# One load for three inverse tiles, score stacks issued four rounds later, and a late projection in the bank of the sums: a change to a kernel of two attention and two spectral layers

## The chip, the cores and the metric

The kernel runs on one core of a Trainium2 chip. A core has five engines that each work through a queue of their own in order: TensorE (PE in the profile, its weight loads PEld), VectorE (DVE), ScalarE (ACT), GpSimd (POOL) and SyncE (SP). Here SP computes nothing: it issues nearly all transfers between the chip's main memory (DRAM) and the core's own memory. The metric is device time in microseconds (us), the median of several runs. Before the change it is 1366.31 us, from three runs of 1366.28 to 1366.6 us.

## The reference

The input `x` has 2048 tokens of 576 columns. Two kinds of layers alternate, each added to its input: attention in a sliding window of 256 tokens with 32 heads of 18 columns, and a spectral filter (a two-dimensional Fourier transform, a product with a complex filter, the transform back).

```python
def _A_ref(x, wqkv, wo):
    H = 32; Dh = D // H; W = 256
    qkv = (x @ wqkv).reshape(B, S, 3, H, Dh).transpose(2, 0, 3, 1, 4)
    q, k, v = qkv[0], qkv[1], qkv[2]
    scores = jnp.einsum("bhqd,bhkd->bhqk", q, k) * (Dh ** -0.5)
    mask = (idx[:, None] - idx[None, :] >= 0) & (idx[:, None] - idx[None, :] < W)
    p = softmax(jnp.where(mask, scores, -1e9))
    o = jnp.einsum("bhqk,bhkd->bhqd", p, v)
    return o.transpose(0, 2, 1, 3).reshape(B, S, D) @ wo

def _B_ref(x, w_r, w_i):
    X = jnp.fft.rfft2(x, axes=(-2, -1)) * (w_r + 1j * w_i)
    return jnp.fft.irfft2(X, s=(S, D), axes=(-2, -1))

x = A_x
x = x + _A_ref(layernorm(x), A_wqkv, A_wo)
x = x + _B_ref(layernorm(x), B_w_r, B_w_i)
x = x + _A_ref(layernorm(x), A_wqkv, A_wo)
x = x + _B_ref(layernorm(x), B_w_r, B_w_i)
```

Everything is fp32. The kernel splits a number into a high part that TensorE multiplies exactly and a low part, the remainder, and adds the products of the parts.

## The kernel before

**Attention layer.** The 2048 tokens are 16 tiles of 128, the 32 heads are 8 quads of 4. First come the layer norm and the projection of the values (L1005). Then the queries and keys are projected: `proj(i, c)` computes column group `i` (of 9) for token block `c` (of 4, 512 tokens each) in 14 TensorE steps into one bank of PSUM, the memory that TensorE writes its products to. ScalarE copies the high part out (`sg`), and the remainder (`tensor_sub`, L1127) is put in a list `ended`, which `remainders()` empties later on VectorE. After it a DMA (L1129) stores both parts to DRAM (`qk_d`). The bank is free when the remainder is done.

From DRAM they come back arranged for the scores: `stack_load(n, c)` issues 12 loads (L1144, six for queries `qs`, six for keys `ks`) that build the stack of quad `n`, block `c`. There are two buffers, used by even and odd quads in turn.

The work on a quad runs in rounds, one for each of its 16 tiles, 128 rounds in all. A round has four score products (`score_max`, L1169), which VectorE reduces to row maxima (L1171), and, ten rounds later (`LEAD = 10`), four exponent products (`exps`, L1206), which ScalarE turns into probabilities (L1207). GpSimd cuts the window out of them, and TensorE adds up the products with the values (`part`, L1226) in a bank named `U`. After each four rounds `m_rows(n, c)` transposes the maxima, ScalarE negates them (`mt`, L1184), and four small DMAs (L1189) write them as one more row of `qs`, so that the next exponent products of that block subtract them. `norm` divides the sums and stores them (L1251).

**PSUM.** The banks go by tags: three of tag `S` for scores, three of tag `E` for exponent products, one `pj` for projections and one `U` for the sums. In the first ten rounds, the opening, there are no exponent products yet: the projections take turns in `pj` and the `E` banks (column group 2), and the fourth score of a round uses `U`.

**Order.** `opening()` runs ten rounds of scores with 70 projection steps between them. `bursts()` then takes three exponent products and three scores at a time; the projection steps that are left are spread over bursts by the tables `ends` and `unit`, one projection of 14 steps for each entry of `ends`. The first of these is `proj(3, 0)`, in an `E` bank, then `proj(3, 1)`, in `pj`. After 118 rounds (`MIX`) a loop without scores follows.

`loads(t)` runs at the start of round `t` of the exponent products (rounds below are in this count) and issues stacks: those of quad 1 at rounds -4, 4, 8 and 12, those of quads 2 to 7 at every fourth round, with the quad and block of round `t + 20`. `behind(t)` runs after a round, for the layer's end: at round 104 the output weights (`room`, L734, two loads to `ofree`), at rounds 107, 109 and so on the constants of the next stage (`const`, L748, `dc`), later the layer's input rows. All of these stand in SP's one queue, which issues in order; a load that must wait for data holds up those behind it. SP's DMAs signal on eight semaphores in turn, so that each also waits for the eighth before it.

**Spectral layer.** After the forward transform a pipeline of 16 groups `g` applies the filter along the tokens (L496, L517); VectorE and GpSimd write the result `ze`, and each group's rows are stored to DRAM (`yd`, L554). The inverse transform then works through 16 tiles `n2` (L591 and after). Its tile `n2` needs rows of all groups: tiles 0 to 2 get the rows of groups 0 to 10 by loads from `yd` that are issued in groups 10 and 13 (L544, three loads each time, one for each tile), and the rows of later groups straight from `ze` (L524). Tile 3 and later ones are fetched whole from `yd` (`fetch`, L585), and the layer's input is loaded in pairs of tiles (`ld`, L170). All these tiles lie in the room `ofree`, called `rl` in the code; `yis` are its four places for inverse tiles, one behind the other from column 4640 on, and `near` is 3.

Of the kernel before, what the change touches and what calls it, by code (L numbers as in the profile page):

```python
# [136 lines left out]
def layer_b(tc, xf, dst, dcs, gc, ident, rh, rl, out, ga_d, fc_d, m2_d, w_d, wo_d, wo2_d, dram, nxt, share):  # L137
# [10 lines left out]
    with ExitStack() as stack:  # L148
# [361 lines left out]
        def g2(g, h):  # L510
# [30 lines left out]
            if g in (FG - 1, FG + 2):  # L541
                lo, hi = (0, 8) if g < FG else (8, FG)
                for n2 in range(near):
                    nc.sync.dma_start(yis[n2][8 * lo:8 * hi].rearrange("p c f -> p (c f)"), yd[1][n2, lo:hi].rearrange("g i f -> (g i) f"))  # L544
            if g == 14:
# [30 lines left out]
        def ly(n2, h):  # L576
            h["y"] = yis[n2 % 4]
            if n2 == 0:
                ld(4)
            for k in (near,) if n2 == 0 else (n2,) if n2 > near + 1 else ():  # L580
                fetch(k)

        def fetch(k):
            if k >= near:
                nc.sync.dma_start(yis[k % 4].rearrange("p c f -> p (c f)"), yd[1][k].rearrange("g i f -> (g i) f"))  # L585
# [279 lines left out]
def layer_a(tc, ident, eps, bp, src, dst, wqk_d, wv_d, wo_d, dc_d, gc_d, dram, copy, wvs, second, spectral, share):  # L865
# [17 lines left out]
    if True:  # L883
# [192 lines left out]
        with ExitStack() as c2:  # L1076
# [17 lines left out]
            def remainders():  # L1094
                while ended:
                    ended.pop(0)()

            def proj(i, c, bank=0):
# [5 lines left out]
                def mm(s, k):  # L1104
# [3 lines left out]
                    if s == 0:  # L1108
                        box["ps"] = pp.tile([128, 512], F32, tag="E" if bank else "pj", name=f"pj{i}_{c}", bufs=3 if bank else 1)
                    w = wt[i][0] if p == "h" else wt[i][1]  # L1110
# [153 lines left out]
            LEAD = 10  # L1264
            pj = [f for i in range(2, 9) for c in range(4) for f in proj(i, c, c % 2 if i == 2 else c == 0 and i == 3)]
            done, due = 0, []
# [3 lines left out]
            def loads(t):  # L1270
                if t + LEAD in (0, 2):
                    stack_load(0, 2 + (t + LEAD) // 2)
                if t in (-4, 4, 8, 12):
                    stack_load(1, max(t, 0) // 4)
                n, c = divmod(t + 20, NT)
                if c % 4 == 0 and 1 < n < NQ:
# [33 lines left out]
            def bursts():  # L1310
# [4 lines left out]
                values = {(4 * x + 7) // 3 + 2 for x in range(0, MIX - 2, 2)}  # L1315
                ends = [3] + [max(k - 1 for k in values if k - 1 <= 4 + 134 * (i + 1) // 22) for i in range(22)]
                unit = {k: i for i, end in enumerate(ends) for k in range(ends[i - 1] + 1 if i else 0, end + 1)}
# [99 lines left out]
            for f in opening():  # L1417
                f()
                done += 1
            U = pp.tile([128, 512], F32, tag="U", name="U", bufs=1)  # L1420
            V.memset(U, 0.0)
            for f in bursts():
# [96 lines left out]
```

## Time and profile before

| | before |
|---|---|
| median of 3 runs | 1366.31 us |
| the profiled execution, its own time | 1367.9 us |
| its span, first to last instruction | 1366.2 us |
| mean granted TensorE clock | 0.997 |
| TensorE busy, attention layer 1 (0 to 490 us) | 481.6 of 490.0 us |
| TensorE busy, spectral layer 1 (490 to 705 us) | 211.2 of 215.0 us |
| TensorE busy, attention layer 2 (705 to 1186 us) | 473.4 of 481.0 us |
| TensorE busy, spectral layer 2 (1186 to 1366.2 us) | 169.7 of 180.2 us |
| chain that ended last: TensorE / DMA / VectorE / ScalarE | 87% / 4% / 3% / 2% |
| score products (L1169), idle time of TensorE just before them | 1.0 us |
| exponent products (L1206), idle time of TensorE just before them | 6.4 us |

The table's windows come from the view that sums an engine's busy time over a stretch. How to read the rows of the other views:

- A row of the timeline has the start in us, the duration in us, the engine, the line of the kernel, the operation, the tile written and the tiles read, the shapes and how many instructions of one kind stand together (x6). `SPq` is SP's queue: the duration of such a row is the time in which the DMAs were issued, not the time until the data is there. In brackets stands how long the engine had been idle before, and what ended the idle time.
- A row of the table of waits has the engine, the tile and line that waited, what it waited for, and then three numbers: the total in us, the number of waits, and the longest of them. It also sums only waits in a given stretch where one is asked for.
- The granted clock is TensorE's, 1.00 at full speed.

### The profile page before, as it was taken

Reading aid. Unit: us, or ns where it says so; the run is one execution under the profiler, and the core shown is the slowest. Engines: PE = TensorE matmul, PEld = TensorE weight load, DVE = VectorE, ACT = ScalarE, POOL = GpSimd, SP = SyncE. Lnnn points to the kernel's source line nnn. Section 1 sums busy time; section 2 is a strip of 40 time slices with the busy share of each in tenths; the row PEclk is TensorE's granted clock in tenths of the full one; section 3 lists DMA queues with packets and bytes.
Section 4 is the critical chain, followed back from the end, with each engine's and each line's share of the span. In section 5 each row is a group of like instructions: output and inputs, shape, how many; then the busy total and the mean of one; then the engine's idle time right before and its main releaser. Section 6 shows DMA issues by size and latency. Waiting matters only on the chain.

```text
span 1366.2 us, 33609 instructions
## 1 busy us (share of the span) xinstructions
PE 1335.8 (98%) x11351; PEld 997.2 (73%) x11351; DVE 900.5 (66%) x3060; ACT 780.0 (57%) x1966; POOL 644.0 (47%) x1154
## 2 busy tenths in 40 slices
PE   9999999999999999999999999999999999999998
PEld 8986666666665699975999965566666655898587
DVE  5418777877778376666663157777777785576745
ACT  5522777777778544542455316677777778464223
POOL 3257545555546533476221394455455458213721
PEclk9999999999999999999999999999999999999999
DMA  6756665655446457778773467555555555597875
GB/s 204 208 164 194 207 190 166 188 166 160 150 145 180 129 154 249 223 237 266 253 243 73 114 194 224 160 170 162 153 158 153 157 157 168 143 359 253 301 234 173
DMA packets 202425, 259.11 MB, mean 190 GB/s; under 512 B 104599, under 2 KB 109975, under 8 KB 201743
## 3 DMA queue, kind: packets, MB, share of 16 engines
q1 hardware_dynamic: 191551, 235.72, 57.0%
q10 hardware_dynamic: 7648, 14.96, 3.1%
q0 software_dynamic: 3056, 6.28, 1.8%
q8 instruction: 92, 1.51, 0.5%
q14 instruction: 78, 0.64, 0.2%
HBM read 156.11 MB, written 101.01 MB: 188 GB/s over the span
## 4 chain that ended last, share of the span: by engine, by line
PE 87%; DMA 4%; DVE 3%; ACT 2%; issue 2%; SPq 1%; POOL 0%; ACTq 0%; DVEq 0%; POOLq 0%
PE pj L1112 19%; PE S L1169 12%; PE U L1226 12%; PE vps L1005 8%; PE ops L800 7%; PE E L1206 6%; PE po L257 3%; PE pq L517 2%; PE tpo L1240 2%; PE pf L257 2%; PE p L496 2%; PE pi L591 2%; PE pz L295 2%; DMA ofree<-yd 1%; PE tpm L1182 1%
## 5 line engine op out<-in xcount | busy, mean ns | idle before, releaser
L1171 DVE CUSTOM_DVE_ANT_0 jk<-S,mask 128x384 bf16<-128x384 f32 (+2 forms) x1024 | 490.7, 529 | 113.5 <-PE E L1206 60.3
L1207 ACT ACTIVATE P<-E 128x384 f32<-128x384 f32 (+2 forms) x1024 | 409.1, 476 | 128.0 <-PE E L1206 99.2
L1209 POOL TENSOR_SCALAR_AFFINE_SELECT P<-P 128x512 f32<-128x512 f32 x256 | 162.6, 635 | 278.2 <-ACT P L1207 257.3
L1169 PE MATMUL S<-ks,qs 63*128 63x384 f32 (+2 forms) x1024 | 269.1, 371 | 1.0 <-DMA qs<-qk_d 0.4
L1206 PE MATMUL E<-qs,ks 64*128 64x384 f32 (+2 forms) x1024 | 222.4, 372 | 6.4 <-DMA qs<-mt 3.7
L1169 PEld LDWEIGHTS S<-ks,qs 63*128 63x128 f32 x1024 | 140.7, 185 | 105.4 <-DVE m L1171 72.4
L1226 PE MATMUL U<-P,vq 128*19 128x128 f32 (+1 forms) x3840 | 188.3, 329 | 0.6 <-DVE us L1231 0.2
L1112 PE MATMUL pj<-xh,wqh 128*128 128x512 f32 x360 | 156.2, 434 | 1.7 <-DVE sg L1127 1.3
L1226 PEld LDWEIGHTS U<-P,vq 128*19 128x19 f32 x3840 | 96.0, 98 | 77.7 <-issue 25.0
L1212 POOL TENSOR_SCALAR_AFFINE_SELECT P<-P 128x512 f32<-128x512 f32 x224 | 142.3, 635 | 0.0
L1206 PEld LDWEIGHTS E<-qs,ks 64*128 64x128 f32 x1024 | 113.7, 185 | 21.3 <-ACT P L1207 9.7
L1112 PE MATMUL pj<-xh,wql 128*128 128x512 f32 x360 | 124.4, 418 | 0.0
L1112 PE MATMUL pj<-xl,wqh 128*128 128x512 f32 x288 | 122.3, 425 | 0.0
L800 PE MATMUL ops<-oroom 128*128 128x290 f32 (+1 forms) x812 | 115.4, 298 | 0.4 <-DVE ofree L846 0.2
L800 PEld LDWEIGHTS ops<-oroom 128*128 128x128 f32 x812 | 110.2, 189 | 1.1 <-DVE ofree L823 0.7
L1112 PEld LDWEIGHTS pj<-xh,wqh 128*128 128x128 f32 x360 | 67.8, 188 | 32.5 <-issue 10.5
L1171 DVE DVE_READ_ACCUMULATOR2_ANT m<- 128x1 f32 x1024 | 85.3, 83 | 0.0
L1127 DVE TENSOR_TENSOR sg<-pj,sg 128x512 fp32r<-128x512 f32 x72 | 49.5, 687 | 52.5 <-ACT sg L1124 52.5
L1124 ACT CAST sg<-pj 128x512 fp32r<-128x512 f32 x72 | 42.2, 586 | 69.2 <-PE pj L1112 54.2
L1112 PEld LDWEIGHTS pj<-xh,wql 128*128 128x128 f32 x360 | 64.3, 189 | 20.3 <-issue 10.7
L1005 PE MATMUL vps<-wvh,xh 128*128 128x288 f32 x320 | 71.4, 304 | 0.0
L1112 PEld LDWEIGHTS pj<-xl,wqh 128*128 128x128 f32 x288 | 54.3, 189 | 18.3 <-issue 11.6
(599 smaller groups left out, 2257.5 us busy)
## 6 DMA issues: line engine op xcount, KB each, us to landing
qk_d<-sg SPq DMA_DIRECT2D x56, 512.0 KB
qs<-qk_d SPq DMA_DIRECT2D x384, 72.0 KB
ks<-qk_d SPq DMA_DIRECT2D x348, 72.0 KB
v_d<-vt SPq DMA_DIRECT2D x32, 304.0 KB
vq<-v_d SPq DMA_DIRECT2D x16, 608.0 KB
wt<-in_w SPq DMA_DIRECT2D x16, 580.0 KB
ofree<-x SPq DMA_DIRECT2D x16, 580.0 KB
x<-ofree SPq DMA_DIRECT2D x32, 290.0 KB
```

Of the source, the lines that this page charges most:

```text
L257: T.matmul(ps[:, c, 0:NF], tail[r] if si == 4 else hl_(si), dcs[b // 2][r, b % 2], start=mi == si == 0, stop=si == 4)
L800: self.nc.tensor.matmul(self.ps[u][n][:, 0:self.n], x, self.w[p][:, (2 * wk + n) * self.n:(2 * wk + n + 1) * self.n], start=first and i == ...
L1005: T.matmul(ps[:, n, 0:288], xT(xk, c), w[:, wk, n * 288:(n + 1) * 288], start=i == 0, stop=i == len(ks) - 1)
L1112: T.matmul(box["ps"].rearrange("r (n p) -> r n p", n=NT) if second else box["ps"], w[:, wk], x, start=s == 0, stop=s == len(ks) - 1)
L1127: V.tensor_sub(rest[:, 1], by, rest[:, 0].bitcast(F32))
L1169: T.matmul(ps[:, 0:N], q[b:b + 63, pair, i * 128:i * 128 + 128], k[b:b + 63, pair, lo:hi], start=True, stop=True)
L1171: V.tensor_tensor_reduce(out=jk[:, 0:N], in0=ps[:, 0:N], in1=mask[:, 384 - N:384], scale=1.0, scalar=-3e38, op0=ALU.add, op1=ALU.max, accu ...
L1206: T.matmul(ps[:, 0:nq], k[b:b + 64, pair, j * 128:j * 128 + 128], q[b:b + 64, pair, j * 128:j * 128 + nq], start=True, stop=True)
L1207: A.activation(p[:, hl_, 0:nq], ps[:, 0:nq], AF.Exp, scale=SC)
L1209: P.affine_select(out=p[:, :, 0:128], in_=p[:, :, 0:128], pattern=[[0, 4], [1, 128]], compare_op=ALU.is_ge, fill=0.0, base=0, channel_mult ...
L1212: P.affine_select(out=p[:, :, 256:384], in_=p[:, :, 256:384], pattern=[[0, 4], [-1, 128]], compare_op=ALU.is_gt, fill=0.0, base=0, channel ...
L1226: T.matmul(U[32 * h:32 * h + 19, (q0 % 4) * 128:(q0 % 4) * 128 + 128 * (q1 - q0)], vts[n][:, j, h], pt[n, j][:, h, (q0 - j) * 128:(q1 - j) ...
```

## The change

There are four edits. The bulk loads of the first three inverse tiles become one DMA that writes all three tiles (in groups 10 and 13). In the first tile of the inverse transform the fetch of tile 3 is issued ahead of the load of the input pair 4. The projection `proj(3, 0)` goes to the bank `pj` instead of an `E` bank, and `proj(3, 1)` to `U`, which therefore exists earlier, with a `remainders()` ahead of it and without the memset; the first entry of `ends` is 2 instead of 3. The stacks of quads 2 to 7 are those of round `t + 16` instead of `t + 20`.

```diff
@@ spectral layer, group g of the filter along the tokens @@
             if g in (FG - 1, FG + 2):
                 lo, hi = (0, 8) if g < FG else (8, FG)
-                for n2 in range(near):
-                    nc.sync.dma_start(yis[n2][8 * lo:8 * hi].rearrange("p c f -> p (c f)"), yd[1][n2, lo:hi].rearrange("g i f -> (g i) f"))
+                nc.sync.dma_start(rl[8 * lo:8 * hi, 4640:4640 + 580 * near].rearrange("p (n f) -> p n f", n=near),
+                                  yd[1][0:near, lo:hi].rearrange("n g i f -> (g i) n f"))
@@ spectral layer, tile n2 of the inverse transform @@
             h["y"] = yis[n2 % 4]
+            for k in (near,) if n2 == 0 else (n2,) if n2 > near + 1 else ():
+                fetch(k)
             if n2 == 0:
                 ld(4)
-            for k in (near,) if n2 == 0 else (n2,) if n2 > near + 1 else ():
-                fetch(k)
@@ attention layer, proj @@
-                        box["ps"] = pp.tile([128, 512], F32, tag="E" if bank else "pj", name=f"pj{i}_{c}", bufs=3 if bank else 1)
+                        box["ps"] = U if bank == 2 else pp.tile([128, 512], F32, tag="E" if bank else "pj", name=f"pj{i}_{c}", bufs=3 if bank else 1)
@@ attention layer, the list of projection steps @@
-            pj = [f for i in range(2, 9) for c in range(4) for f in proj(i, c, c % 2 if i == 2 else c == 0 and i == 3)]
+            pj = [f for i in range(2, 9) for c in range(4) for f in proj(i, c, c % 2 if i == 2 else 2 if (i, c) == (3, 1) else 0)]
@@ attention layer, loads @@
-                n, c = divmod(t + 20, NT)
+                n, c = divmod(t + 16, NT)
                 if c % 4 == 0 and 1 < n < NQ:
                     stack_load(n, c // 4)
@@ attention layer, bursts @@
-                ends = [3] + [max(k - 1 for k in values if k - 1 <= 4 + 134 * (i + 1) // 22) for i in range(22)]
+                ends = [2] + [max(k - 1 for k in values if k - 1 <= 4 + 134 * (i + 1) // 22) for i in range(22)]
@@ attention layer, between opening and bursts @@
             for f in opening():
                 f()
                 done += 1
+            remainders()
             U = pp.tile([128, 512], F32, tag="U", name="U", bufs=1)
-            V.memset(U, 0.0)
             for f in bursts():
```

Three places show how this moves the loads in SP's queue. In the rows, a number behind a tile's name numbers its buffer, and `x4` says how many instructions of one kind stand together.

The first place is SP's queue in the first attention layer, rounds 12 to 16. `mt1_0` is the row of maxima of quad 1, block 0, which is written to the odd quads' buffer `qs1`; `qs1`/`ks1` from `qk_d` are a stack of quad 1, `qs0`/`ks0` a stack of quad 2; `sg3_3` is the store of a projection. Before:

```order
L1189 DMA qs1_1060<-mt1_0_2134 1x4x128 x4
L1144 DMA qs1_1060<-qk_d_83 18x2x512 x6
L1144 DMA ks1_1061<-qk_d_83 18x2x512 x6
L1144 DMA qs0_1058<-qk_d_83 18x2x512 x6
L1144 DMA ks0_1059<-qk_d_83 18x2x512 x6
L1129 DMA qk_d_83<-sg3_3_2228 128x2x512
L1251 DMA o_d_85<-o0_2_2311 128x4x72
L1189 DMA qs1_1060<-mt1_1_2342 1x4x128 x4
```

With the change:

```order
L1189 DMA qs1_1060<-mt1_0_2132 1x4x128 x4
L1144 DMA qs1_1060<-qk_d_83 18x2x512 x6
L1144 DMA ks1_1061<-qk_d_83 18x2x512 x6
L1129 DMA qk_d_83<-sg3_3_2214 128x2x512
L1251 DMA o_d_85<-o0_2_2297 128x4x72
L1189 DMA qs1_1060<-mt1_1_2328 1x4x128 x4
L1144 DMA qs0_1058<-qk_d_83 18x2x512 x6
L1144 DMA ks0_1059<-qk_d_83 18x2x512 x6
```

The first stack of quad 2 has moved from ahead of the row `mt1_1` to behind it, past a store of a projection and one of an output.

The second place is SP's queue at the end of the same layer, rounds 104 to 111, where the last stacks are those of quad 7. `ofree` from `in_wo` are the output weights, `dc0` and `dc1` the first two constants, `mt7_0` and `mt7_1` the rows of maxima of quad 7, `o6_1` an output. Before:

```order
L1144 DMA qs1_1060<-qk_d_83 18x2x512 x6
L1144 DMA ks1_1061<-qk_d_83 18x2x512 x6
L734 DMA ofree_7004<-in_wo 128x1152
L734 DMA ofree_7004<-in_wo 128x1728
L1189 DMA qs1_1060<-mt7_0_7098 1x4x128 x4
L1251 DMA o_d_85<-o6_1_7140 128x4x16
L1251 DMA o7_d_86<-o6_1_7140 128x4x56
L748 DMA dc0_7144<-dcr_62 128x580
L748 DMA dc1_7239<-dcr_62 128x580
L1189 DMA qs1_1060<-mt7_1_7273 1x4x128 x4
```

With the change:

```order
L1144 DMA qs1_1060<-qk_d_83 18x2x512 x6
L1144 DMA ks1_1061<-qk_d_83 18x2x512 x6
L734 DMA ofree_6990<-in_wo 128x1152
L734 DMA ofree_6990<-in_wo 128x1728
L1189 DMA qs1_1060<-mt7_0_7084 1x4x128 x4
L1251 DMA o_d_85<-o6_1_7126 128x4x16
L1251 DMA o7_d_86<-o6_1_7126 128x4x56
L748 DMA dc0_7130<-dcr_62 128x580
L1144 DMA qs1_1060<-qk_d_83 18x2x512 x6
L1144 DMA ks1_1061<-qk_d_83 18x2x512 x6
L748 DMA dc1_7237<-dcr_62 128x580
L1189 DMA qs1_1060<-mt7_1_7271 1x4x128 x4
```

The stack ahead of the weights is now the last but one; the last stack stands between the constants `dc0` and `dc1`, ahead of the row `mt7_1`.

The third place is SP's queue in the first spectral layer, where the filter along the tokens ends and the inverse transform begins. `yd1` is the DRAM tensor of the stored rows, `eo2`, `ze13`, `eo3` and `ze15` are rows of groups 12, 13, 14 and 15, and `x0` is the layer's input. Before:

```order
L524 DMA ofree_7004<-eo2_8122 8x580 x2
L544 DMA ofree_7004<-yd1_8102 24x580 x3
L524 DMA ofree_7004<-ze13_10155 8x580
L524 DMA ofree_7004<-eo3_8123 8x580
L524 DMA ofree_7004<-ze15_10188 8x580 x2
L554 DMA yd1_8102<-ze13_10155 16x8x580
L554 DMA yd1_8102<-ze15_10188 16x8x580
L170 DMA ofree_7004<-x0_59 128x1160 x2
L585 DMA ofree_7004<-yd1_8102 128x580 x2
```

With the change:

```order
L524 DMA ofree_6990<-eo2_8120 8x580 x2
L543 DMA ofree_6990<-yd1_8100 24x3x580
L524 DMA ofree_6990<-ze13_10151 8x580
L524 DMA ofree_6990<-eo3_8121 8x580
L524 DMA ofree_6990<-ze15_10182 8x580 x2
L554 DMA yd1_8100<-ze13_10151 16x8x580
L554 DMA yd1_8100<-ze15_10182 16x8x580
L170 DMA ofree_6990<-x0_59 128x1160
L585 DMA ofree_6990<-yd1_8100 128x580
L170 DMA ofree_6990<-x0_59 128x1160
L585 DMA ofree_6990<-yd1_8100 128x580
```

Three loads of group 13 have become one, and the fetch of tile 3 (the first L585) stands ahead of the second load of input rows instead of behind it.

## The prediction

> **What bounds the kernel now.** I read the page first, for its share of busy time, then the table of waits for TensorE, then TensorE's granted clock in short windows, and last the timeline of SP (the queue that issues nearly every transfer) at each place where TensorE stood still.
>
> ```profile
> span 1366.2 us, 33609 instructions
> PE 1335.8 (98%) x11351; PEld 997.2 (73%) x11351; DVE 900.5 (66%) x3060; ACT 780.0 (57%) x1966; POOL 644.0 (47%) x1154
> ```
>
> TensorE is busy for 98% of the span, so 30.4 us of idle time is all that an edit of order can win there, and the change removes no matmul. The waits, longest first:
>
> ```profile
> PE E L1206 <- DMA qs<-mt: 3.7, 2, 2.5
> PE pi L591 <- DMA ofree<-ze: 3.4, 2, 2.0
> PE pi L591 <- DMA ofree<-yd: 2.0, 2, 1.5
> ```
>
> Each is one event in each layer: the exponent products wait for a row of maxima, the inverse transform waits for its last rows and then for its fourth tile. Two of these waits have a tail, which only the clock shows (columns: window, busy time of PE, PEld, DVE, ACT, POOL, then granted clock, DMA share, GB/s):
>
> ```profile
> 643.20:647.00 3.80, 3.80 (x15) 3.24 (x14) 2.24 (x5) 0.00 (x0) 1.39 (x6) 0.56 0.97 301
> 879.40:882.70 3.30, 3.30 (x25) 1.58 (x23) 1.61 (x6) 1.33 (x4) 1.03 (x2) 0.52 0.64 201
> ```
>
> At a clock of 0.56 the first stretch loses 3.80 x 0.44 = 1.7 us, the second 3.30 x 0.48 = 1.6 us. They are the only such stretches while TensorE works, and each follows a gap of 2.0 us or more (rows below).
>
> **Term 1, stacks four rounds later.** In round 12 SP issues two stacks, 24 loads, ahead of the four small loads that carry a row of maxima. In the second layer:
>
> ```profile
> 865.38 3.21 SPq L1144 DMA_DIRECT2D qs<-qk_d  x6
> 868.63 3.29 SPq L1144 DMA_DIRECT2D ks<-qk_d  x6
> ...
> 873.50 2.73 SPq L1189 DMA_DIRECT2D qs<-mt  x4
> ...
> 866.39 0.27 ACT L1184 ACTIVATE mt<-tpm 16x128 fp32r<-16x128 f32 x1
> ...
> 877.26 0.90 PE L1206 MATMUL E<-qs,ks 64*128 64x384 f32 x3 [2.49 <-DMA qs<-mt]
> ...
> 179.01 1.03 PE L1206 MATMUL E<-qs,ks 64*128 64x384 f32 x3 [1.21 <-DMA qs<-mt]
> ```
>
> The row was ready at 866.66 and was issued 6.8 us later, behind the second stack of 6.5 us. With that stack in round 16 the row leaves some 6.5 us earlier, more than both waits: 2.49 + 1.21 = 3.7 us gone, and with the gap the stretch at half clock, 1.6 us. Together **5.3** (bounds 3.7 to 5.3). Round 16 then holds one stack, as it does now.
>
> **Term 2, the projections' banks.** The last projection of the opening sat in one of the three E banks until VectorE had taken its remainder:
>
> ```profile
> 128.90 0.44 PE L1206 MATMUL E<-qs,ks 64*128 64x384 f32 x1 [0.68 <-ACT P L1207]
> 131.62 0.44 PE L1206 MATMUL E<-qs,ks 64*128 64x384 f32 x1 [0.44 <-ACT P L1207]
> ...
> 130.37 0.69 DVE L1127 TENSOR_TENSOR sg<-pj,sg 128x512 fp32r<-128x512 f32 x1
> ...
> PE E L1206 <- ACT P L1207: 1.0, 2, 0.5
> ```
>
> Until 131.06 only two E banks turned; that cost 1.1 us here and 1.0 us (the last row, the waits between 780 and 835 us) in the second layer. Now this projection has the pj bank and the next one the bank of sums, so three turn at once. The remainder moves ahead of the round's reductions on VectorE, which delays each score by up to 0.69 us; three S banks cover that. The bank of sums must be read out before the sums start, a whole burst after the projection ends. Bounds 0 to 2.1; I take **1.7**, near the upper end, since the buffer that was lacking is there. The memset that goes was hidden behind TensorE.
>
> **Term 3, the inverse transform, first layer.** SP is the chain here: three loads, then four short ones, the last two with the rows that the first inverse product needs.
>
> ```profile
> 635.20 2.28 SPq L544 DMA_DIRECT2D ofree<-yd  x3
> ...
> 639.08 1.38 SPq L524 DMA_DIRECT2D ofree<-ze  x2
> ...
> 637.13 0.45 DVE L529 TENSOR_TENSOR ze<-pq,both 128x290 f32<-128x290 f32 x1
> ...
> 642.31 0.97 PE L591 MATMUL pi<-ofree,ga 128*128 128x290 f32 x3 [2.00 <-DMA ofree<-ze]
> ```
>
> One load in place of three takes no less than one of them (2.28 / 3 = 0.76) and no more than all three; I take 0.8, as SP's time goes by instructions in these rows. Then 1.5 us are free, but the last rows can't leave before VectorE has written them at 637.58: 639.08 - 637.6 = 1.4 us won. The gap of 2.00 falls to 0.6 us, shorter than any that the half clock followed, so its 1.7 us go too: **3.1** (bounds 0 to 3.7).
>
> **Term 4, the same place in the second layer.**
>
> ```profile
> 1295.35 1.21 SPq L544 DMA_DIRECT2D ofree<-yd  x3
> ...
> 1298.15 1.33 SPq L524 DMA_DIRECT2D ofree<-ze  x2
> ...
> 1296.81 0.45 DVE L529 TENSOR_TENSOR ze<-pq,both 128x290 f32<-128x290 f32 x1
> ...
> 1302.30 0.97 PE L591 MATMUL pi<-ofree,ga 128*128 128x290 f32 x3 [1.38 <-DMA ofree<-ze]
> ...
> 1305.14 0.80 SPq L585 DMA_DIRECT2D ofree<-yd  x2
> ...
> 1310.77 0.51 PE L591 MATMUL pi<-ofree,ga 128*128 128x290 f32 x1 [1.54 <-DMA ofree<-yd]
> ```
>
> Three take 1.21, so 0.8 is saved, and VectorE's rows are ready at 1297.26: 0.8 of the 1.38 goes. The fourth tile landed 5.6 us after its issue, with two loads of 580 KB ahead of it; one of them now stands behind it, which at this place's pace is worth more than the 1.54 us waited. I take 1.2 of 1.54, since it must still wait for the last store. **2.0** (bounds 0 to 2.9). In the first layer this load has slack.
>
> **Term 5, what the shift costs.** The last stack of a layer moves from ahead of the output weights' loads (L734) to between the first two constants, and so ahead of the next row of maxima:
>
> ```profile
> 416.73 2.12 SPq L1144 DMA_DIRECT2D qs<-qk_d  x6
> 418.89 2.35 SPq L1144 DMA_DIRECT2D ks<-qk_d  x6
> 421.33 0.84 SPq L734 DMA_DIRECT2D ofree<-in_wo  x2
> ...
> 427.99 2.33 SPq L748 DMA_DIRECT2D dc<-dcr  x2
> 430.42 2.44 SPq L1189 DMA_DIRECT2D qs<-mt  x4
> ...
> 434.75 1.21 PE L1206 MATMUL E<-qs,ks 64*128 64x384 f32 x3
> ...
> 1129.90 2.51 SPq L748 DMA_DIRECT2D dc<-dcr  x2
> 1132.51 2.44 SPq L1189 DMA_DIRECT2D qs<-mt  x4
> ...
> 1135.46 1.06 PE L1206 MATMUL E<-qs,ks 64*128 64x384 f32 x3
> ```
>
> The second constant waits until the weights have landed, about 430; twelve loads take 4.5 us, and they will stand there too. Part returns: the stack at 416.73 had waited 2.2 us for the last projection's store; its successor, with other columns, needs it only at its sixth load, so the weights come some 1.8 us sooner (in the second layer 1.1). So the four small loads are 2.7 us late in the first layer and 3.4 in the second. Their slack is read from the rows: issued by 432.86 and used at 434.75, 1.9 us; by 1134.95 and used at 1135.46, 0.5 us. In term 1's rows TensorE went on 1.0 us after the last issue (876.23 to 877.26). So 0.9 us are spare in the first layer and none in the second: waits of 1.8 and 3.4 us, queued ahead of every later score, product and sum, since TensorE takes them in order. The longer one may bring a half-clock stretch of 1.6 us; at even chance 0.8. Loss **6.0** (bounds 0 to 10.6: no lead returned, both clocks halved).
>
> **Sum.** 5.3 + 1.7 + 3.1 + 2.0 - 6.0 = 6.1 us off the span of 1366.2: 1360.1. The median, 1366.31, lies 0.1 above this span (the profiled execution itself took 1367.9), so the forecast is **1360.2** for the median.
>
> The Trainium skill (TensorE: Matmul & The Clock Gate, Part 1) has the clock halve after an idle window of about 3.4 us. In these rows gaps of 2.00 and 2.49 us were enough and 1.38 and 1.54 were not; I go by the rows. By the page's figure the two gaps would be too short to cause the stretches.
>
> **Rivals.**
> (a) The stack at the end of the layer is hidden, its load landing sooner than the rows say: term 5 is zero, 1366.3 - 12.1 = 1354.2. For it: slack exists in the first layer; against: 0.5 us in the second.
> (b) One load of three tiles holds SP as long as three did: terms 3 and 4 shrink to the 1.2 us of the order of loads, 1366.3 - 8.2 + 6.0 = 1364.1. The change then doesn't do what it says. For it: issues in those rows differ from 0.40 to 0.76 us each, so their cost is not understood.
> (c) The half-clock stretches have another cause and stay: 3.3 us less, 1363.5. For it: the second begins 2.1 us after its gap has ended.
> (d) Term 5 is paid in full, 10.6 us, in both layers: 1366.3 - 12.1 + 10.6 = 1364.8.
> (e) The other side: the stacks come too late for their scores, at all 24 of a layer.
>
> ```profile
> 295.38 2.23 SPq L1144 DMA_DIRECT2D qs<-qk_d  x6
> ...
> 319.95 0.44 PE L1169 MATMUL S<-ks,qs 63*128 63x384 f32 x1
> ...
> 337.92 2.42 SPq L1144 DMA_DIRECT2D qs<-qk_d  x6
> ```
>
> Stack (5,0) starts at 295.38 and is first read at 319.95; sixteen rounds take 42.5 us (to 337.92), so four take 10.6, and 14 us are left, of which 4.5 are issue. It decides once SP lags or a load lands 9 us later than it seems. Then each of 48 stacks waits, at 0.5 us each 24 us: 1366.3 - 12.1 + 24 = 1378. Against it: SP had gaps there and the margin is twice the issue.
>
> **Numbers.** Forecast 0.58, with its own range 1356.5 to 1363.4; (a) 0.14, (b) 0.08, (c) 0.06, (d) 0.06, (e) 0.08. A measurement of this kernel tells about 0.2%, 2.7 us, from no change. The forecast, (a) and (c) are faster by more: 0.78; (b) and (d) lie within: 0.14; (e) is slower: 0.08. The range reaches from (a) to past (d): 1354 to 1365.5, which leaves out (e), and parts of the rest.
>
> **What would show it.** Right: no wait of exponents for qs<-mt near 178 and 875, but a new one near 430 and 1130, ahead of the first sums of constants; granted clock 1.0 after the inverse's first product in the first layer; E waits of L1206 on ACT gone at the bursts' start. Wrong: one L543 issue of 2 us, a score that waits for DMA ks<-qk_d in the middle of a layer, or no new wait at the end of it.

## The result, and the profile after

The changed kernel is slower. Its median is 1373.4 us (5 runs, 1371.23 to 1373.65) against 1366.31 us before (5 runs, 1364.25 to 1366.6), a ratio of 1.0050 with an interval of 1.0034 to 1.0066. The forecast was 1360.2 us. Run twice more, each time beside the kernel before on the same chip, it came to 1.0021 (1.0004 to 1.0038) and 1.0037 (1.0023 to 1.0050): 3 to 7 us slower, never faster.

The profiled execution of the changed kernel took 1373.65 us. Its page:

```profile
span 1371.9 us, 33652 instructions
PE 1341.0 (98%) x11351; PEld 998.4 (73%) x11351; DVE 900.0 (66%) x3058; ACT 778.7 (57%) x1966; POOL 643.7 (47%) x1154
```

TensorE's idle time is 1371.9 - 1341.0 = 30.9 us, where it was 30.4. Not one microsecond of waiting was won in sum. Its busy time rose by 5.2 us with the same 11351 products, and that is nearly all of the 5.7 us by which the span grew. The same products took longer, so the clock comes next. The windows of the changed kernel in which it was halved (columns as in the prediction, the clock third from the end):

```profile
434.41:441.24 6.83, 6.83 (x44) 3.49 (x46) 3.14 (x12) 3.20 (x9) 1.22 (x2) 0.50 0.49 148
840.60:847.43 6.83, 6.83 (x50) 3.69 (x47) 2.95 (x12) 3.38 (x9) 3.94 (x5) 0.50 0.46 155
1137.56:1144.39 6.83, 5.71 (x38) 2.78 (x39) 3.13 (x12) 2.78 (x7) 1.22 (x2) 0.50 0.54 154
1311.64:1315.05 3.41, 3.41 (x13) 2.84 (x12) 1.04 (x3) 0.84 (x2) 0.69 (x3) 0.50 0.97 329
```

Before there were 6.8 us at half clock ahead of the end (two stretches of 3.4); now there are 6.83 x 3 + 3.41 = 23.9. The longest waits of TensorE, from the table of waits:

```profile
PE E L1206 <- ACT P L1207: 2.4, 4, 1.7
PE pi L591 <- DMA ofree<-ze: 1.9, 2, 1.5
PE wo L257 <- DVE et L251: 1.9, 1, 1.9
PE S L1169 <- DMA qs<-mt: 1.9, 1, 1.9
PE S L1169 <- DMA ks<-qk_d: 1.8, 1, 1.8
```

All but the first tile's part of the second row stand where the kernel before had no wait of that length, and each half-clock stretch begins within 0.8 us of the end of one. Place by place, the timelines show what came in the place of each wait that was removed.

**End of the first attention layer.** SP's queue and the product that waited:

```profile
414.32 2.14 SPq L1144 DMA_DIRECT2D ks<-qk_d  x6
416.60 1.39 SPq L734 DMA_DIRECT2D ofree<-in_wo  x2
418.08 2.44 SPq L1189 DMA_DIRECT2D qs<-mt  x4
420.75 1.59 SPq L1251 DMA_DIRECT2D o_d<-o  x2
423.15 0.33 SPq L748 DMA_DIRECT2D dc<-dcr  x1
425.23 2.12 SPq L1144 DMA_DIRECT2D qs<-qk_d  x6
427.39 2.25 SPq L1144 DMA_DIRECT2D ks<-qk_d  x6
429.72 0.35 SPq L748 DMA_DIRECT2D dc<-dcr  x1
430.17 2.77 SPq L1189 DMA_DIRECT2D qs<-mt  x4
```

```profile
433.89 0.41 PE L1169 MATMUL S<-ks,qs 63*128 63x384 f32 x1 [1.86 <-DMA qs<-mt]
```

The weights did come sooner (416.60 instead of 421.33), and the row of maxima was issued at 430.17, where it had been 430.42. But TensorE is ahead by then: it comes to this product at 432.03, where the kernel before had it at 434.74. What waits is a score product, which is the first that needs the last stack; that stack was issued from 425.23 to 429.64. The name behind the arrow is the last landing that the profile saw, and the row and the stack landed close together, so that the row's own lateness is covered here. In the second layer both are late, one behind the other:

```profile
1137.03 0.40 PE L1169 MATMUL S<-ks,qs 63*128 63x384 f32 x1 [1.84 <-DMA ks<-qk_d]
1138.68 0.65 PE L1206 MATMUL E<-qs,ks 64*128 64x384 f32 x1 [1.25 <-DMA qs<-mt]
```

**Opening of the second attention layer.** The two waits of 0.5 us on the E banks are gone, and a longer one stands more than 10 us later, in the first bursts:

```profile
829.27 2.78 SPq L1144 DMA_DIRECT2D qs<-qk_d  x6
835.07 3.13 SPq L1129 DMA_DIRECT2D qk_d<-sg  x4
...
839.36 0.87 ACT L1207 ACTIVATE P<-E 128x384 f32<-128x384 f32 x2 [2.44 <-DMA qk_d<-sg]
839.90 0.82 PE L1206 MATMUL E<-qs,ks 64*128 64x384 f32 x2 [1.68 <-ACT P L1207]
```

ScalarE may not write its probabilities (`P`) before a projection's store has left the same buffer (`sg` of the first twelve projections lies in tag `P`, six buffers in turn), and that store stood behind a stack on SP.

**Inverse transform, first layer.** The bulk load takes 0.41 us of SP and the wait for the rows falls from 2.00 to 0.42, as forecast. Then `et`, an operand of later products, is late:

```profile
637.16 0.41 SPq L543 DMA_DIRECT2D ofree<-yd  x1
...
643.69 1.22 PE L591 MATMUL pi<-ofree,ga 128*128 128x290 f32 x4 [0.42 <-DMA ofree<-ze]
646.03 0.69 DVE L251 TENSOR_TENSOR et<-tp,et 128x512 fp32r<-128x512 f32 x1 [5.83 <-DMA yd<-ze]
646.78 1.46 PE L257 MATMUL wo<-dc,et 128*128 128x290 f32 x9 [1.88 <-DVE et L251]
```

VectorE waits for the stores of `ze` to land before it may write `et`. Before, it waited for the same stores, under the cover of the wait for the rows:

```profile
643.20 0.69 DVE L251 TENSOR_TENSOR et<-tp,et 128x512 fp32r<-128x512 f32 x1 [4.97 <-DMA yd<-ze]
```

**Inverse transform, second layer.** Tiles 0 and 1 start without a wait, then tile 2 waits for rows that GpSimd's queue issues:

```profile
1306.16 2.12 PE L591 MATMUL pi<-ofree,ga 128*128 128x290 f32 x8
...
1309.40 0.46 PE L245 MATMUL tp0q<-ident,tl 128*99 128x128 f32 x2 [0.68 <-POOL tl L236]
1311.34 1.02 PE L591 MATMUL pi<-ofree,ga 128*128 128x290 f32 x2 [1.48 <-DMA ofree<-ze]
```

### The profile page after: what moved, and what is told of

It is laid out like the page before. It is cut to its first block, busy times and chain, and to the rows that moved or that the text cites. A ratio compares the mean times of both kernels' runs of the same rounds, so it can differ in the third digit from the quotient of the medians.

```text
span 1371.9 us, 33652 instructions
## 1 busy us (share of the span) xinstructions
PE 1341.0 (98%) x11351; PEld 998.4 (73%) x11351; DVE 900.0 (66%) x3058; ACT 778.7 (57%) x1966; POOL 643.7 (47%) x1154
## 4 chain that ended last, share of the span: by engine, by line
PE 87%; DMA 5%; DVE 3%; ACT 2%; issue 2%; SPq 1%; POOL 0%; DVEq 0%; ACTq 0%; POOLq 0%
PE pj L1112 18%; PE U L1226 12%; PE S L1169 12%; PE vps L1005 8%; PE ops L800 7%; PE E L1206 6%; PE po L257 4%; PE pq L517 2%; PE tpo L1240 2%; PE p L496 2%; PE pf L257 2%; PE pi L591 2%; PE pz L295 2%; DMA qk_d<-sg 1%; DMA yd<-ye 1%
## 5 line engine op out<-in xcount | busy, mean ns | idle before, releaser
L1226 PE MATMUL U<-P,vq 128*19 128x128 f32 (+1 forms) x3840 | 191.2, 332 | 0.9 <-DVE m L1171 0.3
L1112 PE MATMUL pj<-xh,wqh 128*128 128x512 f32 x350 | 151.7, 433 | 1.1 <-DVE sg L1127 0.7
L1112 PE MATMUL pj<-xh,wql 128*128 128x512 f32 x350 | 121.6, 421 | 0.0
L1112 PE MATMUL pj<-xl,wqh 128*128 128x512 f32 x280 | 118.7, 424 | 0.0
```

The costliest lines, as they stand in the source:

```text
L1112: T.matmul(box["ps"].rearrange("r (n p) -> r n p", n=NT) if second else box["ps"], w[:, wk], x, start=s == 0, stop=s == len(ks) - 1)
L1226: T.matmul(U[32 * h:32 * h + 19, (q0 % 4) * 128:(q0 % 4) * 128 + 128 * (q1 - q0)], vts[n][:, j, h], pt[n, j][:, h, (q0 - j) * 128:(q1 - j) ...
```

## The experiments

Theory at the start: the waits were removed where they stood, the next late thing took their place, and the half clock behind the new, longer waits made the loss. Rival: the loss belongs to a single edit, or to one execution. Each run below has its own profile, and up to 12 timed executions beside the kernel before on the same chip.

**Each edit alone.** `stacks_alone` has only `divmod(t + 16, NT)` on the kernel before, `banks_alone` only the edits of `proj`, `pj`, `ends` and `U`, `inverse_alone` only those of L544 and `ly`.

> Only the fourth edit: stacks of quads 2 to 7 at t + 16. Theory (the loss sits where the last stack of each layer lands late, and in the half clock behind it): round 18 wins 6.2 us in the two layers, as the two traces show it (the exponent products' offset there falls by 1.7 and 4.5), the end of the two layers loses 10.3 (4.8 and 5.5): 4 us slower than before, about 1370.4, with two half-clock stretches near 434 and 1137 us. Rival (the loss belongs to the other edits, the stacks are a gain as predicted or nothing): 1360 to 1366.

> Only the third edit: the two late projections in pj and in the bank of the sums. Theory (the stall of 1.68 us in the opening of the second layer, with its half clock, is this edit's doing: TensorE comes sooner to a P tile whose store still runs): 0.7 us won in the first layer, 3.8 lost in the second, about 1369.4. Rival (that stall came from the timing of the stores in that execution, not from the edit): the waits of 1.1 and 1.0 us at the bursts' start go and nothing else: 1364.5 to 1365.

> Only the first two edits: one bulk load, and the fetch ahead of the input pair. Theory (the first inverse tile's wait goes and the next late thing takes its place: the tile et in the first layer, the rows of tile 2 from GpSimd's queue in the second): 2.0 us won in the first layer, within 0.5 in the second: 1364 to 1365. Rival (the prediction's terms 3 and 4 hold when nothing else is changed): 5 us won, 1361.

Measured: stacks 1.0019 (1.0007 to 1.0031), banks 1.0010 (0.9993 to 1.0026), inverse 0.9997 (0.9981 to 1.0013). No edit is a gain. The fourth, forecast at +0.7 us (terms 1 and 5), costs 2.6 us (0.0019 of 1364.1); the others, forecast at -1.7 and -5.1, can't be told from nothing. In their profiles each wait stands where theory had it, though smaller than in the first trace: the stacks alone wait 0.97 and 0.80 us at the first score of the last stack, the banks alone 0.77 us for the store in the second layer. Of the inverse edits alone, the table of waits shows that the first layer's wait has moved as a whole:

```profile
PE pi L591 <- DMA ofree<-ze: 2.0, 2, 1.6
...
PE wo L257 <- DVE et L251: 1.7, 1, 1.7
```

**The last stacks ahead of the weights again** (`last_early`):

```diff
-                if c % 4 == 0 and 1 < n < NQ:
+                if c % 4 == 0 and 1 < n < NQ and t < 100 + 4:
                     stack_load(n, c // 4)
+                if t in (103, 104):
+                    stack_load(7, t - 101)
```

> The changed kernel, but the last two stacks of a layer go out at rounds 103 and 104, ahead of the output weights as before. Theory (the loss at a layer's end comes from the last stack): both stalls near 434 and 1137 us and their half clock go, 10.3 us less than the changed kernel, about 1363. Rival (the row of maxima behind the constants is late by itself, or the half clock has another cause): the stalls stay, 1371 to 1373.

Measured: 1376.26 us, 1.0101 (1.0083 to 1.0120), the worst of all. The waits at the first score of the last stack are gone, and the weights, now behind two stacks, hold ScalarE, which splits them ahead of its probabilities (L741):

```profile
429.75 0.67 ACT L741 CAST oroom<-ofree 128x576 fp32r<-128x576 f32 x1 [3.07 <-DMA ofree<-in_wo]
...
430.65 0.77 PE L1206 MATMUL E<-qs,ks 64*128 64x128 f32 x3 [2.10 <-ACT P L1207]
```

In the changed kernel the stack that stands behind the weights on SP is late, in this one the weights that stand behind the stacks; the kernel before left both room, and so does another order, further below (`tail_alone`).

**The row on another queue** (`row_on_act`), to tell whether the row or the stack was late:

```diff
-                        (nc.sync if n or c > 1 else nc.scalar).dma_start(...)
+                        (nc.scalar if n == 0 and c < 2 or (n, c) == (7, 1) else nc.sync).dma_start(...)
```

> The changed kernel, but the row of maxima 1 of quad 7 is issued on ScalarE's queue, so that it doesn't stand behind the last stack. Theory (the last stack itself lands late): the first score of that stack still waits 1 to 2 us in both layers, only the second wait of the second layer (1.25 us, exponent products on qs<-mt) goes: 0 to 2 us less than the changed kernel. Rival (the prediction: the row behind the stack is what comes late): both stalls go, 8 to 10 us less.

In the first layer the first score of the last stack waits as before, longer even, with the row no longer on SP:

```profile
427.43 2.61 SPq L1144 DMA_DIRECT2D qs<-qk_d  x6
430.08 2.15 SPq L1144 DMA_DIRECT2D ks<-qk_d  x6
...
436.65 0.41 PE L1169 MATMUL S<-ks,qs 63*128 63x384 f32 x1 [2.91 <-DMA dc<-dcr]
```

So there the stack is late by itself, without the row that I had forecast. In the second layer no such wait is left in this execution; in both layers there is a new one of 1.57 us for ScalarE, whose queue now issues the row. The time is no better: 1.0056 (1.0037 to 1.0075).

**Work in the wait** (`filled`), with the changed kernel again beside it (`changed_again`):

```diff
+                    if k == 152:
+                        ps = pp.tile([128, 512], F32, tag="pj", name="fill", bufs=1)
+                        for _ in range(7):
+                            T.matmul(ps[:, 0:128], ident, ident, start=True, stop=True)
                     score_max(*c[0])
```

> The changed kernel again, beside the three below. If the stalls of its trace are its own: a wait of 1 to 2 us in both layers at the first score of the last stack (near 434 and 1137 us) and a wait of exponent products on ScalarE near 838 us, and a ratio to before of 1.003 to 1.007. If they belong to one execution: other places, and a ratio within 0.2%.

> The changed kernel with 7 products of the identity matrix, some 1.5 us, on TensorE ahead of the first score of the last stack, written to a bank that nobody reads. Theory (a wait of TensorE of 1.3 us or more within one of the 3.41 us windows makes the next one or two run at half clock): the wait at that score shrinks by 1.5 us, the half-clock stretches near 434 and 1137 us go, and with them 2 us in each layer: 4 us less than the changed kernel. Rival (the half clock doesn't come from the wait): the stretches stay, and the time is the same or up to 2 us more.

The clock did what theory said: with work in its place no wait over 0.5 us is left at the end of either layer, and the clock there stays at full speed.

```profile
425.00:445.00 20.00, 19.78 (x211) 11.45 (x210) 16.47 (x69) 16.05 (x43) 13.80 (x19) 1.00 0.59 167
1125.00:1150.00 25.00, 24.06 (x253) 13.61 (x253) 17.76 (x72) 19.86 (x52) 17.63 (x25) 1.00 0.66 205
```

The time did not: 1.0027 (1.0015 to 1.0039) against 1.0021 (1.0004 to 1.0038) without the filler. The 4 us are not there. `changed_again` shows why that could be: in its profile the waits at the same place are 1.21 and 1.03 us, and no half clock follows them in that execution, so filler, which took 1.8 us, costs more there than it saves. Nor was the clock cured as a whole: the profile of `filled` has 13.65 us at half clock at other places (from 142.0, 647.2 and 1268.4 us), and the mean clock of its executions was 0.9965 against 0.9959. Of what I expected of `changed_again`, the waits at the last stack came, the one on ScalarE near 838 us did not (0.2 us), and the ratio lies below the 1.003 that I gave.

**Only the double stack taken apart** (`spread_all`: the first three edits, `t + 20`, and the first two stacks of quad 2 in rounds 15 and 17):

> The changed kernel's first three edits, and in place of the fourth: only the first two stacks of quad 2 move, from rounds 12 and 16 to 15 and 17; all others stay at t + 20. Theory (the double stack of round 12 made the row late, and the shift's loss lies at the layer's end alone): no wait of exponent products for qs<-mt near 178 and 875 us, none at the layer's end; 10 us less than the changed kernel, 3 to 5 less than before. Rival (the gain at round 18 is given back elsewhere): within 2 us of before.

The time is 1.0009 (0.9996 to 1.0022): no loss that can be told, and no gain. The waits at round 18 and at the layers' end are gone; another row stands behind the moved stacks:

```profile
202.22 0.41 PE L1206 MATMUL E<-qs,ks 64*128 64x384 f32 x1 [1.42 <-DMA qs<-mt]
```

**The kernel before once more, and two causes taken away at their source.** `stores_on_act` is `banks_alone` with `i < 3` for `i < 2` in the choice of the store's queue; `rows_on_pool` is the kernel before with `nc.gpsimd` for `nc.sync` at L1189; `mended` has the third edit and both.

> The kernel before, for a second profile of it. Theory (the waits that the prediction took from one execution were larger than most): the waits of exponent products for qs<-mt at round 18 sum to less than 3 us in the two layers instead of 3.7, the waits of E on ScalarE at the bursts' start are 1.0 in each layer again, those of the inverse transforms 2 us in the first layer and 1.5 to 3 in the second; at most one half-clock stretch ahead of the end. Rival (they are the kernel's own): 3.4 to 4 us at round 18, two stretches.

> The third edit alone, and with it the four stores of column group 2 on ScalarE's queue instead of SP's. Theory (the new wait in the opening is for the store of such a projection, which stands in SP's queue behind a stack, since its buffer becomes a P tile): the waits of E on ScalarE between 120 and 146 us and between 812 and 846 fall below 0.3 us in both layers; 1 to 3 us less than the third edit alone, 0 to 2 less than before. Rival (the wait has another cause, such as VectorE's remainder): 0.5 to 1.7 us of it stay.

> The kernel before, with the rows of maxima issued on GpSimd's queue, so that no stack stands ahead of them. Theory (what the shift of the stacks was to win can be had without it): no wait of exponent products for qs<-mt in the middle of a layer nor at its end; 1 to 4 us less than before. Rival (GpSimd's queue is later than SP's, behind the selects that wait for ScalarE): waits for qs<-mt in many rounds, 5 us more or worse.

> The third edit with the stores of column group 2 on ScalarE's queue and the rows of maxima on GpSimd's, the rest as before. If both hold: the sum of the two runs above, 2 to 6 us less than before. If the waits only move again: within 1 us of before.

The kernel before shows the same waits again at round 18, 3.6 us in sum, 3.36 of them in the second layer, and two half-clock stretches: there the rival was right, and the waits that the prediction took recur. With the stores on ScalarE's queue no wait of an exponent product is left in either opening, so the store behind the stack was the cause. But the opening's scores now wait instead, ahead of the first exponent product (the table of waits between 118 and 146 us, and between 812 and 846):

```profile
PE S L1169 <- DVE m L1171: 1.4, 1, 1.4
...
PE S L1169 <- DMA qs<-mt: 3.2, 1, 3.2
```

The time of `stores_on_act` is 1.0019 (1.0009 to 1.0030), not below the third edit alone. With the rows on GpSimd's queue no wait for `qs<-mt` is left in the table of waits; instead TensorE waits for GpSimd, whose select now comes behind the rows' issues:

```profile
451.32 0.41 PE L1226 MATMUL U<-P,vq 128*19 128x128 f32 x8 [2.12 <-POOL P L1209]
```

That gives 1.0040 (1.0022 to 1.0059), and both together 1.0043 (1.0027 to 1.0060).

**The fourth edit split.** `tail_alone` moves only the last stack of a layer to round 108. `head_alone` moves quads 2 to 6 to `t + 16` and puts quad 7 in rounds 95, 97, 100 and 104; `head_inverse` adds the first two edits.

> Only the start of the fourth edit: the stacks of quads 2 to 6 at t + 16, those of quad 7 in rounds 95, 97, 100 and 104, so that the last one stands ahead of the output weights as before. Theory (the start wins what the waits at round 18 cost, the end loses more): no wait for qs<-mt at round 18, none at the layers' end, mean clock as before: 1 to 3.5 us less than before (ratio 0.9975 to 0.9993). Rival (the gain at the start is given back later, whatever the end does): ratio 0.9995 or more.

> Only the end of the fourth edit: the last stack of a layer in round 108 instead of 104, all others at t + 20. Theory (the end is the cost): the first score of that stack waits 0.8 to 1.9 us in each layer, with half clock behind it in some executions: 2 to 5 us more than before (ratio 1.0015 to 1.0037), mean clock lower by 0.001 to 0.003. Rival (the end costs nothing on the median): ratio below 1.001.

> The whole change once more, beside the three others. Theory: a ratio of 1.002 to 1.005, a mean clock 0.002 to 0.004 below that of before, and at equal clock no difference over 1 us.

> The start of the fourth edit with the first two edits (one bulk load, fetch ahead of the input pair). Theory (the first two edits win nothing, since the tile et and the rows from GpSimd's queue come next): as head_alone, within 1.5 us. Rival (they win once the rest does not disturb): 2 us or more below head_alone.

Here my theory of the layer's end fell. The last stack in round 108 alone costs nothing: 0.9999 (0.9983 to 1.0015), and no wait stands at its first score. On SP the weights leave first, and the last stack finds the queue free:

```profile
413.85 0.95 SPq L734 DMA_DIRECT2D ofree<-in_wo  x2
...
424.23 2.18 SPq L1144 DMA_DIRECT2D qs<-qk_d  x6
426.45 2.62 SPq L1144 DMA_DIRECT2D ks<-qk_d  x6
...
433.76 0.44 PE L1169 MATMUL S<-ks,qs 63*128 63x384 f32 x1
```

In the changed kernel another stack stood ahead of the weights, which left at 416.60, and TensorE, ahead by what round 18 had saved, came to that score earlier. The second weighs more: the last stack was issued by 429.64 there and by 429.07 here, 0.6 us apart, and TensorE came to its first score at 432.03 there and at 433.76 here, 1.7 us apart. In the second layer the two differences are 0.2 and 1.75 us. `head_alone` is no gain either, 1.0022 (1.0005 to 1.0040), but it tells less than it should: three stacks close together brought a new late row.

```profile
395.19 0.41 PE L1206 MATMUL E<-qs,ks 64*128 64x384 f32 x1 [1.81 <-DMA qs<-mt]
```

`head_inverse` gave 1.0034 (1.0021 to 1.0047), with the same new wait.

**The shift kept, the end relieved.** Both kernels put the stacks 1 and 2 of quad 7 in rounds 99 and 101, so that none stands ahead of the weights.

> The fourth edit alone, but the stacks 1 and 2 of quad 7 in rounds 99 and 101 instead of 100 and 104, so that no stack stands ahead of the output weights. Theory (the end costs through the row of stack, weights and last stack on SP's queue): the waits of 0.8 to 1 us at the first score of the last stack go or fall below 0.5, and with round 18 free of its wait the time is 1 to 3 us below before (ratio 0.998 to 0.9995), 2.5 to 5 below the fourth edit as it is. Rival (the shift of the middle costs): ratio 1.001 or more.

> The whole change with the same two stacks moved. Theory: the wait at the first score of the last stack falls below 0.5 us; 2 to 4 us less than the whole change (which stood at 1.002 to 1.005), so a ratio of 0.9995 to 1.002. Rival (the time goes to waits that move, wherever they are taken away): 1.002 to 1.005 again, with the wait at another place.

The wait at the last stack is gone in both, and yet both are slower than the fourth edit as it is (1.0019): 1.0046 (1.0031 to 1.0061) and 1.0048 (1.0033 to 1.0063). The row behind the moved stacks is late by more:

```profile
420.25 1.02 PE L1206 MATMUL E<-qs,ks 64*128 64x384 f32 x2 [2.90 <-DMA qs<-mt]
```

No kernel of these beats the kernel before; `inverse_alone` and `tail_alone` are level with it, and for `banks_alone` and `spread_all` no loss can be told.

## Why the prediction was wrong

Three profiles of the changed kernel can be set against the two of the kernel before. The table gives how many microseconds the changed kernel wins (-) or loses at each place: the difference of the start of the same TensorE instruction in the two traces behind the place, less that ahead of it. The first column of traces is the pair of the prediction, the others are `changed_again` and `changed_third` against `before_again`.

| place, both layers together | forecast | first pair | second | third |
|---|---|---|---|---|
| openings and first bursts (term 2) | -1.7 | +3.1 | +2.9 | -0.3 |
| round 18 (term 1) | -5.3 | -6.7 | -6.5 | -6.5 |
| end of the attention layers (term 5) | +6.0 | +9.6 | +3.5 | +8.1 |
| inverse, first layer (term 3) | -3.1 | -1.7 | -1.5 | -1.6 |
| inverse, second layer (term 4) | -2.0 | +0.3 | -1.3 | +0.4 |
| all, with what lies between | -6.1 | +5.7 | -0.9 | +1.3 |

In the first pair, which is one draw, the forecast was off by 11.8 us: 4.8 in term 2, 3.6 in term 5, 1.4 and 2.3 in terms 3 and 4, 1.1 between the places, less 1.4 that term 1 won beyond its forecast. The step that failed is the same in terms 2 to 4: each counted the wait that it removed as won, without asking which other operand of the next products was late. In term 5 it is the clock behind the waits, and the stack itself, which the sum did not price.

**Term 1 was right against these two executions of the kernel before.** The double stack made the row late and moving it took the wait and its half clock away. It need not be the gain of a typical execution: in the six profiles that have the same double stack, with the rows on SP, the waits there sum to 0.7, 1.4, 2.2, 3.5, 3.6 and 3.7 us, and the last two are those of the kernel before. The profiled execution of `before_again` took 1367.03 us where the median of its 12 was 1365.27.

**Term 5: the price of the waits was close, what waits first and the clock were not.** I forecast waits of 1.8 and 3.4 us at this place; 1.86 and 1.84 + 1.25 stand there. But the product that stops first, in both layers, is the score that needs the last stack. The step that fell is the assumption that a stack four rounds later still had room, so that only the row behind it had a price. I had tested that room in the middle of a layer, 14 us, and rival (e) with it; at the end, behind the weights, it was gone. The row's lateness itself came in the first layer about as forecast, 2.7 us: it was issued by 432.94, where it had been 432.86, with TensorE 2.7 us ahead; there the wait for the stack covers it, and in the second layer 1.25 us of it are left. The larger error is the clock: 1.6 us at even chance, once. Both waits were followed by 6.83 us at half clock, and with them the place lost 9.6 us. That lies below the upper bound, which I gave as 10.6; its own terms (3.6 and 4.5 us of waits, twice 1.6 of clock) make 11.3. The split showed that the end alone is not enough for the waits: without the rest of the shift, which brings TensorE there 1.7 us sooner and puts a stack ahead of the weights, there were none.

**Term 2 failed behind "three turn at once".** The E banks do turn three at once, and the two waits of some 0.5 us in each opening are gone. But in the nine profiles that have the third edit with the stores on SP, 0 to 1.1 us are left in the first layer, in one piece, and in the second a wait on ScalarE took their place in all but one of them, from 0.6 to 1.7 us in one piece. In the first pair that wait and the half clock behind it turned the term into a loss of 3.1 us. I had named VectorE and the bank of sums as what could be late next, not the buffer of the probabilities. A row of the kernel before had shown it, ScalarE waiting for that store under cover:

```profile
837.39 0.87 ACT L1207 ACTIVATE P<-E 128x384 f32<-128x384 f32 x2 [0.78 <-DMA qk_d<-sg]
```

The 2.9 us of the second pair have another cause. In `changed_again` that wait is 0.2 us; exponent products wait for a row of maxima instead, and 3.41 us at half clock follow from 854.4 us on:

```profile
852.31 0.97 PE L1206 MATMUL E<-qs,ks 64*128 64x384 f32 x2 [1.01 <-DMA qs<-mt]
```

**Terms 3 and 4 failed in what comes next.** The bulk load won on SP what I said, and rival (b) fell with its 0.41 us. But I asked for the next late thing only on the chain that I had followed. In the first layer `et` stood ready to wait 1.9 us for the same stores; in the second it was the rows of tile 2 on GpSimd's queue. In the first layer 1.5 to 1.7 us are left of 3.1, mostly the half clock; in the second nothing can be told.

**What makes the time.** In sum the waits stayed as they were (30.9, 28.2 and 29.0 us of idle time in the three profiles of the changed kernel, 30.4 and 29.1 in the two before), and the clock went down. Over the timed executions the mean granted clock was 0.9959 (12 executions) against 0.9986 (27) in the second set, and 0.9941 (8) against 0.9986 (31) in the third. In straight lines fitted to the spans, 0.001 of mean clock is worth 1.0 to 1.5 us (0.001 of the span is 1.4), and at a clock of 0.998 the changed kernel lies at 1363.4 against 1363.8, and at 1362.0 against 1363.9. So at equal clock it is no slower (in the third set faster by 1.9 us, where I had expected no difference over 1); all of its loss goes along with the clock. That is a relation over executions, not an experiment: the one experiment on it, `filled`, cured the clock at its place, not as a whole, and won no time.

**Open:** how much of the fourth edit's 1.0019 comes from its start and how much from its end. Both attempts to keep the start without the end brought waits of their own (1.8 and 2.9 us). The three edits alone add up to 1.0026 (0.0019 + 0.0010 - 0.0003), which with their intervals fits the 1.0021 to 1.0050 of the whole: no run shows that together they cost more than their sum.

## What to carry to other kernels

With TensorE at 98%, nearly every wait that was removed here had another close behind it, on an engine or queue that waited under its cover: before a gain is counted, follow every operand of the next few instructions back, not only the one that came last. Count a gap by its length in one piece as much as by the sum of all gaps: here most gaps of half a microsecond cost their length and no more, while one of 1.5 us may cost twice that through the clock. And where executions differ by as much as the gain that is sought, a wait sized in one profile is one draw; take a second profile of the kernel before, first of all.

## What the runs showed of the hardware

The half-clock stretches of TensorE last 3.41 or 6.83 us, never anything between, ahead of the end of a program. Over the 20 profiles of this study, the share of TensorE's gaps in which a stretch started in the gap or within 3.5 us of its end:

| gap | all | attention | filter along the tokens (L496) |
|---|---|---|---|
| 0.3 to 0.8 us | 6 of 361 | 3 of 120 | 0 of 11 |
| 1.2 to 2.0 us | 17 of 54 | 12 of 23 | 1 of 16 |
| 2.0 us and more | 23 of 28 | 13 of 15 | 2 of 3 |

A gap of 1.2 to 2 us is followed by half clock in about half of the cases in the attention layers, and hardly ever between the filter's products; why these differ is open.

In each trace the stretches begin whole multiples of 3.413 us apart (in the changed kernel's 119, 206 and 257 after the first), and where these windows lie against the program's start differs from trace to trace. TensorE's idle time summed over one such window, at full clock, sorts the cases more sharply than the gap does: with 0.3 to 0.7 us the next window ran at half clock in none of 319 cases, with 0.7 to 2.0 us in 29 of 137, with more in 16 of 17. The wait of 1.21 us in `changed_again` lay on both sides of a boundary, at 434.52 us, and no half clock followed.

The Trainium skill (TensorE: Matmul & The Clock Gate, Part 1) describes a gate that judges TensorE in free-running windows of 3.41 us, which agrees with the lengths and the starts here, and would explain that the same gap is halved in one execution and not in the next. Its idle window of about 3.4 us is not needed: the 1.86 us at 433.89 were enough for two windows at half clock.

The second surprise is the spread. The same kernel on the same chip took 1358.7 to 1370.7 us in 29 executions, so that the intervals of these ratios are as wide as most of the effects.
